# First batch's Fourier transform regrouped by TensorE transposes in place of a round trip through DRAM

## The chip, the cores and the metric

One core of a Trainium2 chip runs the whole program. The metric is device time in microseconds (us) of one execution; the number to compare is the median of several. The five engines are TensorE (PE, matrix multiplies into PSUM), VectorE (DVE), ScalarE (ACT), GpSimd (POOL) and SyncE (SP, which here only issues DMAs). Each engine works through its own instruction queue in order.

## What is computed

There are 8 batches of a 3072 x 256 float32 signal. Each is filtered in the frequency domain and the result goes through two dense layers and a soft mixture of experts:

```python
X = np.fft.rfft(x, axis=1)
y = np.fft.irfft(X * (filt_r + 1j * filt_i), n=3072, axis=1)
h = np.maximum(y.reshape(-1, 256) @ w_in, 0.0)          # 256 -> 2048
x2 = h * h @ w_out                                      # 2048 -> 256
logits = x2 @ phi                                       # 32 slots
# softmax over tokens gathers 32 slot inputs, 8 experts (w1, relu, w2) act on
# them, softmax over slots spreads the slot outputs back over the tokens
```

`w_in` and `w_out` arrive as float64 bit patterns and are turned into pairs of float32 on the chip.

## The kernel before

A transform over 3072 = 128 x 24 points is done in two steps. Step A multiplies by a 128-point matrix over the partition axis (`mm_a`, 12 pairs `u` of the 24 columns). Step B multiplies, for each of 64 frequencies, by a small matrix over the 24 columns (`mm_b`, 8 groups `i`), so the 24 columns have to move into the partition axis in between. The kernel does that through DRAM: `evac_a` copies a result of step A from PSUM to SBUF, `store_a` writes it to the DRAM tile `S`, and `load_s` reads it back with the axes exchanged. Then `filt` (DVE) and `join` (POOL) multiply by the filter, `mm_g` is the inverse of step B, `evac_g` (ACT) and `store_g` bring the group to the DRAM tile `G`, and `load_g` reads it with 4 columns per transfer for the inverse of step A (`mm_ai`, then `lead_ai` on ACT and `rest_ai` on DVE), which yields the input `xo` of the dense layers.

The first batch (b = 0) is a prologue: nothing else can run until its first 512 tokens are in `xo`. From then on pairs of dense-layer matrices (`pair`, `layer`) keep TensorE occupied, and the transforms of batches 1 to 7 are interleaved with them.

The order of the prologue is written by hand. `put0(t, fn)` files an event under a planned time `t`; the events are emitted in order of `t`, and each engine's queue gets its instructions in that order. The planned times are an order and no more: an engine waits until data, a buffer or a PSUM bank is there. The constants are `ST` (`B0`, `dB`: start and spacing of the filter groups; `G0`, `Gd`: start of `load_g` and of the step after it), `WI` (load and conversion of the 8 slices of `w_in`) and `WO` (the same for `w_out`).

One conversion of a `w_in` slice (`conv_wi`) is an ACT copy (k = 0), five DVE operations (k = 1 to 5), an ACT copy to `wiH` (k = 6) and a POOL subtraction to `wiL` (k = 7). Its input tile `wt` has 3 buffers, `wa` 3 and `we` 2. In the prologue the temporaries `f4` share 17 buffers of one tag, `u` shares 12, and PSUM tiles `sd` share 8 banks of one tag.

When the prologue is over, `open_main` exchanges the pools, and the first events of the main stream include `conv_wo(0, ...)`, whose `turn_wo` is a TensorE transpose that stands in TensorE's queue after the first two `layer` calls:

```python
WO = [((56.5, 57, W)[n] if n < 3 else W + 2 * n - 4.5,
       [W + max(2 * n + k - 1.5, 0) for k in (-1, -.5, 0, .5, 1, 1.5, 2, 2.5, 3.5, 4)]) for n in range(8)]
```

Of the kernel before, what the change touches and what calls it, by code (L numbers as in the profile page):

```python
# [6 lines left out]
F32 = mybir.dt.float32  # L7
# [8 lines left out]
D = 256  # L16
# [22 lines left out]
def body(tc, x, cA, cAf, fwd, inv, flt, cst, w_in, w_out, phi, w1, w2, out):  # L39
# [22 lines left out]
    def conv_at(t, act0, dve, hl):  # L62
        return [t + act0] + [t + d for d in dve] + [t + h for h in hl]

    SEQ = (.5, .6, .7, .8, .9)
    WI = [(t, conv_at(c, 0, SEQ, (1, 1.5))) for t, c in (
        (.9, 14), (12.1, 19), (24.2, 29.2), (28.2, 35.2), (34.2, 41.2), (40.2, 47.2), (46.2, 53.2), (52.2, 58.2)
    )]
    WO = [((56.5, 57, W)[n] if n < 3 else W + 2 * n - 4.5,
           [W + max(2 * n + k - 1.5, 0) for k in (-1, -.5, 0, .5, 1, 1.5, 2, 2.5, 3.5, 4)]) for n in range(8)]  # L70
    ev0 = defaultdict(list)

# [40 lines left out]
    def fft_events(b, pl, put, A0, dA, TB, TG, n, st):  # L113
        xv = x[b].rearrange("(p n) d -> p n d", n=N2)

        def big():
            return pl().tile([128, 4, D], F32, tag="f4", name="f4", bufs=n["f"])

        def small():
            return pl().tile([128, 2, D], F32, tag="u", name="u", bufs=n["u"])  # L120

        def load_x(sl):
            if b and sl % 2:
                t = st["x2"]
            else:
                t = wide() if b else big()
# [12 lines left out]

        def mm_a(u):  # L140
            p = side()
            if b == 0:
                a = 2 * (u % 2)
                pe.matmul(p, st["ca"], st["x", u // 2][:, a:a + 2, :], start=True, stop=True)
                st["a", u] = p
                return
            h, lo = st.pop(("xs", u))
            pe.matmul(p, ca_t[:, 0, :], h, start=True, stop=False)  # L148
            pe.matmul(p, ca_t[:, 1, :], h, start=False, stop=False)  # L149
            pe.matmul(p, ca_t[:, 0, :], lo, start=False, stop=True)  # L150
            st["a", u] = p

        def evac_a(u):
            if u == 0:
                st["S"] = dram.tile([N1, N2, D], F32, tag="S", name="S")
            p = st.pop(("a", u))
            o = small()
            act.activation(out=o, in_=p.rearrange("p (a d) -> p a d", d=D), func=ACTF.Copy)
            done(p)
            st["o", u] = o  # L160
            if b == 0:
                store_a(u)

        def store_a(u):
            sync.dma_start(out=st["S"][:, 2 * u:2 * u + 2, :], in_=st.pop(("o", u)))
# [5 lines left out]
        def load_w(i):  # L171
            st["fw", i] = w = pl().tile([128, 4, 2, 32], F32, tag="fw", name="fw", bufs=n["c"])
            for r in range(2):
                sync.dma_start(out=w[64 * r:64 * r + 48], in_=fwd[i, 64 * r:64 * r + 48])

        def load_v(i):
            st["iv", i] = v = pl().tile([128, 2, 2, 64], F32, tag="iv", name="iv", bufs=n["c"])
            sync.dma_start(out=v, in_=inv[i])

        def load_f2(j):  # L180
            st["f", j] = f = wide()
# [44 lines left out]
        def load_c(i):  # L226
            w = pl().tile([128, 4, 2, 32], F32, tag="fw", name="fw", bufs=n["c"])
            for r in range(2):
                sync.dma_start(out=w[64 * r:64 * r + 48], in_=fwd[i, 64 * r:64 * r + 48])
            v = pl().tile([128, 2, 2, 64], F32, tag="iv", name="iv", bufs=n["c"])  # L230
            sync.dma_start(out=v, in_=inv[i])
            st["fw", i], st["iv", i] = w, v

        def load_f(i):
            st["f", i] = f = big()
            sync.dma_start(out=f, in_=flt[i])

        def load_s(i):
            st["bi", i] = t = big()
            sv = st["S"].rearrange("(i r c h) n d -> i r (h n) c d", r=2, c=4, h=2)  # L240
            for r in range(2):
                sync.dma_start(out=t[64 * r:64 * r + 48], in_=sv[i, r])

        def mm_b(i):

            t, w = st.pop(("bi", i)), st.pop(("fw", i))
            st["p", i] = p = [side() for r in range(2)]
            for h in range(2):
                for c in range(4):
                    for r in range(2):  # L250
                        rows = slice(64 * r, 64 * r + 48)
                        pe.matmul(  # L252
                            p[r][32 * c:32 * c + 32, D * h:D * h + D], w[rows, c, h, :], t[rows, c, :],
                            start=True, stop=True, tile_position=(64 * r, 32 * c),
                        )

        def filt(i, r):

            p = st["p", i][r]
            f = st["f", i // 2][:, i % 2] if b else st["f", i]  # L260
            for k in range(2):
                st["uv", i, r, k] = u = small()
# [13 lines left out]

        def mm_g(i):
            v = st.pop(("iv", i))
            st["g", i] = p = [side() for c in range(4)]
            y = [st.pop(("y", i, r)) for r in range(2)]  # L280
            for k in range(2):
                for r in range(2):
                    for c in range(4):
                        rows = slice(32 * c, 32 * c + 32)
                        pe.matmul(
                            p[c][64 * r:64 * r + 64, 0:D], v[rows, r, k, :], y[r][rows, k, :],
                            start=(k == 0), stop=(k == 1), skip_group_check=True, tile_position=(32 * c, 64 * r),
                        )

        def evac_g(i, c):  # L290
            if c == 0:
                st["go", i] = big()
# [15 lines left out]

        def warm(a, n):

            p = side()
            w = a.shape[1]
            for _ in range(n):
                pe.matmul(p[:, 0:w], a[:, 0:128], a, start=True, stop=True)

        if b == 0:
# [3 lines left out]
            put(0, load_ca)  # L320
            put(0.05, warm, st["wz"], 2)
            put(0.05, warm, st["wz"][:, 0:256], 1)
            put(18.2, warm, st["ca"], 16)
            for sl in range(6):
                put(0.1 * sl + 0.2, load_x, sl)
            for u in range(12):
                put(4.6 + 0.9 * u, mm_a, u)
                put(6.7 + 1.0 * u, evac_a, u)
            for i in range(8):
                T = ST["B0"] + ST["dB"] * i  # L330
                put((.7, .75, 15)[i] if i < 3 else T - 6.5, load_c, i)
                put((.8, 9, 15.5)[i] if i < 3 else T - 6.4, load_f, i)
                put(18 + .1 * i if i < 3 else T - 6, load_s, i)
                put(T, mm_b, i)
                for r in range(2):
                    put(T + 1 + .5 * r, filt, i, r)
                    put(T + 1 + .5 * r, join, i, r)
                put(T + 5, mm_g, i)
                for c in range(4):
                    put(T + 6, evac_g, i, c)  # L340
                put(T + 7, store_g, i)
            return

        for sl in range(6):
# [458 lines left out]
    def load_const():  # L803
        gps.dma_start(out=ca_t, in_=cA)
        gps.dma_start(out=ss_t, in_=cst[:, C_SS:C_SS + 128])
        sync.dma_start(out=cst_t, in_=cst)
        sync.dma_start(out=phi_t, in_=phi.rearrange("(k p) s -> p k s", p=128))


# [25 lines left out]
    with tc.manual_schedule():  # L835
        put, late = stream("fft"), stream("late")
        st = {}
        put0(38, load_const)
        fft_events(0, lambda: first, put0, 0, 0, 0, 0, dict(f=17, u=12, c=4), st)
        out_events(0, st, late)  # L840
        def wput(t, *a):

# [275 lines left out]
def _constants():  # L1118
# [13 lines left out]
    a[:, 0] = 1.0  # L1132
    a[:, 1] = alt
    cA = np.stack(split(a), axis=1)
    ci = np.where(ri[None, :] == 0, np.cos(ph), -np.sin(ph)).T.copy()
    ci[0] = 1.0
    ci[1] = alt
# [63 lines left out]
    fwd = f2.reshape(8, 2, 4, 64, 2, 32).transpose(0, 1, 3, 2, 4, 5).reshape(8, 128, 4, 2, 32).astype(np.float32)  # L1201
    inv = i2.reshape(8, 2, 4, 32, 2, 64).transpose(0, 2, 3, 1, 4, 5).reshape(8, 128, 2, 2, 64).astype(np.float32)

    cst = np.zeros((128, C_END), np.float32)
    cst[:, C_I:C_I + 128] = ci * (2.0 / N)
# [5 lines left out]
    mats = (cA.astype(np.float32), a.astype(np.float32), fwd, inv)  # L1211
    return [np.ascontiguousarray(m) for m in mats], cst, ks


# [42 lines left out]
```

## Time and profile before

| | us |
|---|---|
| median of 3 runs | 1985.58 |
| lowest and highest | 1982.19, 1985.64 |
| the profiled execution | 1985.45 |
| its span, first to last instruction | 1983.7 |
| first matmul of a dense layer | 99.27 |

The span is what the trace covers; the rest of the profiled execution lies around it. Busy times in the views are sums over instructions of an engine. A row of a timeline or a chain gives the start in us from the beginning of the span, the length in us, and the instruction as engine, line, operation and tiles; "x4" means that four were merged, and what stands in brackets is the idle time ahead and its releaser. [...]

### The profile page before, as it was taken

The numbers are of one execution on the slowest core, as the hardware profiler recorded it, in microseconds if no ns is written. First come the engines' busy times: TensorE is split into PE (matmuls) and PEld (weight loads), VectorE is DVE, ScalarE is ACT, GpSimd is POOL, SyncE is SP. The second block draws the span as 40 slices with busy tenths as digits, with TensorE's granted clock in tenths as the row PEclk, the third lists the DMA queues.
The fourth block names the chain that finished last, engine by engine and source line by source line (L and its number), as shares of the span: only waits on it lengthen the run. The fifth ranks groups of instructions, "written<-read, shape, count | busy, mean of one in ns | idle before, by whom it ended". The sixth has DMA issues, their size and how long they took to land.

```text
span 1983.7 us, 44493 instructions
## 1 busy us (share of the span) xinstructions
PE 1919.6 (97%) x18318; PEld 1313.3 (66%) x18318; DVE 1194.6 (60%) x2230; ACT 1052.1 (53%) x1958; POOL 734.5 (37%) x786
## 2 busy tenths in 40 slices
PE   6799999999999999999999999999999999999987
PEld 3367667666767667667767667667667667676655
DVE  3675665666556655666456655666556656555658
ACT  2256456545645556545645556545655545454535
POOL 1515436343433344343433344343433332222224
PEclk7699999999999999999999999999999999999999
DMA  9833644441342424341342324341342314000589
GB/s 277 238 118 128 174 125 139 124 116 47 130 127 76 109 81 128 89 121 46 130 127 75 104 87 128 83 127 45 131 127 76 97 42 141 13 25 14 164 297 381
DMA packets 144762, 238.29 MB, mean 120 GB/s; under 512 B 14256, under 2 KB 96816, under 8 KB 144560
## 3 DMA queue, kind: packets, MB, share of 16 engines
q1 hardware_dynamic: 144272, 235.26, 39.1%
q8 instruction: 144, 2.36, 0.5%
q14 instruction: 58, 0.48, 0.1%
q0 software_dynamic: 288, 0.20, 0.1%
HBM read 154.66 MB, written 80.74 MB: 119 GB/s over the span
## 4 chain that ended last, share of the span: by engine, by line
PE 89%; DMA 4%; DVE 3%; ACT 2%; issue 2%; SPq 0%; ACTq 0%; DVEq 0%
PE p L442 19%; PE p L444 17%; PE p L443 17%; PE sd L579 10%; PE L L469 9%; PE sd L388 4%; PE sd L252 3%; PE sd L202 3%; DMA wx<-w 1%; PE sd L148 1%; PE sd L149 1%; PE sd L150 1%; DVE ct L912 1%; DMA f<-S 1%; PE pt L901 1%
## 5 line engine op out<-in xcount | busy, mean ns | idle before, releaser
L449 ACT ACTIVATE h<-p 128x512 f32<-128x512 f32 x768 | 459.0, 598 | 561.2 <-PE p L444 546.7
L453 POOL TENSOR_TENSOR h<-h 128x512 f32<-128x512 f32 x383 | 399.9, 1044 | 944.3 <-ACT h L449 899.3
L460 DVE STREAM_TRANSPOSE hT<-h 128x512 f32<-128x512 f32 x768 | 514.1, 693 | 331.0 <-ACT h L451 330.4
L442 PE MATMUL p<-xo,wiH 128*128 128x512 f32 x1536 | 629.5, 410 | 3.0 <-ACT h L449 2.3
L444 PE MATMUL p<-xo,wiL 128*128 128x512 f32 x1536 | 606.8, 395 | 0.0
L443 PE MATMUL p<-xo,wiH 128*128 128x512 f32 x1536 | 606.5, 395 | 0.0
L442 PEld LDWEIGHTS p<-xo,wiH 128*128 128x128 f32 x1536 | 289.6, 189 | 142.1 <-issue 69.9
L444 PEld LDWEIGHTS p<-xo,wiL 128*128 128x128 f32 x1536 | 289.3, 188 | 68.5
L443 PEld LDWEIGHTS p<-xo,wiH 128*128 128x128 f32 x1536 | 289.9, 189 | 57.0 <-DVE xo L409 0.4
L595 DVE SCALAR_TENSOR_TENSOR ac<-ac,sc,sd 128x512 f32<-128x512 f32 x184 | 129.7, 725 | 205.9 <-PE sd L579 205.9
L451 ACT ACTIVATE h<-h 128x512 f32<-128x512 f32 x385 | 243.3, 632 | 12.3
L579 PE MATMUL sd<-hT,eT 32*32 32x512 f32 x6144 | 214.2, 598 | 1.8 <-DVE eT L558 1.8
L272 POOL TENSOR_TENSOR u<-u 128x256 f32<-128x256 f32 x256 | 182.9, 745 | 78.5 <-DVE u L263 71.4
L469 PE MATMUL L<-h,wf 128*32 128x512 f32 x1536 | 186.0, 598 | 0.4 <-ACT h L451 0.4
L579 PEld LDWEIGHTS sd<-hT,eT 32*32 32x32 f32 x6144 | 101.6, 103 | 110.6 <-issue 56.6
L263 DVE TENSOR_TENSOR u<-sd,f 128x512 f32<-128x512 f32 x256 | 158.8, 678 | 21.8 <-PE sd L252 21.1
L137 POOL TENSOR_TENSOR u<-f,u 128x512 fp32r<-128x512 f32 x84 | 108.7, 1295 | 104.4 <-ACT u L136 103.0
L515 DVE TENSOR_TENSOR lo<-L,lp 128x512 fp32r<-128x512 f32 x47 | 32.5, 690 | 134.4 <-ACT lp L514 134.4
L388 PEld LDWEIGHTS sd<-cst_t,gin 128*128 128x128 f32 x768 | 101.4, 193 | 11.4 <-DMA gin<-G 3.2
L212 ACT ACTIVATE f<-sd 128x512 f32<-128x512 f32 x112 | 61.2, 609 | 84.7 <-PE sd L202 84.7
L388 PE MATMUL sd<-cst_t,gin 128*128 128x128 f32 x768 | 102.1, 276 | 2.6 <-DMA gin<-G 2.6
L469 PEld LDWEIGHTS L<-h,wf 128*32 128x32 f32 x1536 | 40.2, 109 | 93.5 <-issue 92.2
(126 smaller groups left out, 1483.1 us busy)
## 6 DMA issues: line engine op xcount, KB each, us to landing
f<-flt SPq DMA_DIRECT2D x28, 1024.0 KB, 6.1
f<-x SPq DMA_DIRECT2D x48, 512.0 KB, 4.9
S<-u SPq DMA_DIRECT2D x96, 256.0 KB, 2.3
f<-S SPq DMA_DIRECT2D x128, 192.0 KB, 7.0
G<-f SPq DMA_DIRECT2D x128, 192.0 KB, 3.1
gin<-G SPq DMA_DIRECT2D x48, 512.0 KB, 5.2
out<-w1t SPq DMA_DIRECT2D x47, 512.0 KB, 5.0
iv<-inv SPq DMA_DIRECT2D x64, 128.0 KB, 4.7
```

The source lines that it names most:

```text
L263: vec.tensor_tensor(out=u, in0=p.rearrange("p (h d) -> p h d", d=D), in1=f[:, 2 * r + k:2 * r + k + 1, :].to_broadcast([128, 2, D]), op=AL ...
L272: gps.tensor_tensor(out=a[:, h, :], in0=a[:, h, :], in1=b[:, 1 - h, :], op=ALU.add if h else ALU.subtract)
L388: pe.matmul(p[:, 128 * a:128 * a + 128], t[:, a, 128 * k:128 * k + 128], cI, start=True, stop=True,)
L442: pe.matmul(p, wh, x[:, 0, kk, :], start=(kk == 0), stop=False)
L443: pe.matmul(p, wh, x[:, 1, kk, :], start=False, stop=False)
L444: pe.matmul(p, wl, x[:, 0, kk, :], start=False, stop=(kk == 1))
L449: act.activation(out=h, in_=p, func=ACTF.Relu, scale=2.0 ** -8)
L451: act.activation(out=h, in_=h, func=ACTF.Square)
L453: gps.tensor_tensor(out=h, in0=h, in1=h, op=ALU.mult)
L460: vec.transpose(hT[c][:, 2 * i + k, :], h2[P, k])
L469: pe.matmul(lg[c][32 * n:32 * n + 32, :], wf[:, f, :], h2.pop((P + n // 2, n % 2)), start=(f < 4), stop=(f >= FT - 4), tile_position=(0, 3 ...
L579: pe.matmul(S[r][32 * t:32 * t + 32, :], e[rows, o:o + 32], h[rows, :, o:o + 32], start=(a == 0), stop=(a == 3), tile_position=(32 * r, 32 ...
```

## The change

The program computes the same. In the first batch the twelve `mm_a` become `mm_at`: the signal is now the stationary operand and the 128-point matrix (its columns reordered on the host, `cAf`) the moving one, so the result comes out with the 256 channels on the partitions; four 128-column multiplies per pair instead of one of 512. `evac_at` copies each result into one SBUF tile `AT`, in runs of two elements that lie 32 elements apart. After the twelfth, `mm_t` takes 4 transposes per half group (16 half groups) and `evac_t` copies each half group to SBUF, on ACT but for two on DVE. `store_a`, `load_s` and `S` are gone for this batch.

Tiles and PSUM banks of the prologue get names (`one`, `bank0`) in place of shared tags. The matrices of step B come in 2 loads of four groups (`load_c`), with a `memset` on POOL for the unused rows, and `mm_b` of this batch reads 64 rows instead of 48. The 16 warming multiplies with `ca` go. `cst` is loaded at the start. The conversions of `w_in` are spread otherwise: slices 0 and 1 ahead of the filters, slice 2 one DVE operation per group, slices 3 to 5 after the last filter, slices 6 and 7 (loaded after `load_g`) after `rest_ai` in DVE's queue. The layout of `fwd` and `inv` in DRAM changes for all batches.

```diff
-    ST = dict(B0=22, dB=4, G0=58.5, Gd=1.5)
+    ST = dict(F0=20.3, dF=2.9, G0=49, Gd=1.5)
+    WI = [
+        conv_at(.4, 8.6, 8.7, 12.3, 12.4),
+        conv_at(.7, 12.5, 12.6, 15.8, 15.9),
+        (1.35, [20.0] + [F(k + 1) + 2.45 for k in range(5)] + [F(6) + 4.4, 44.1]),
+        conv_at(27, 38, 44, 47.2, 47.3),
+        conv_at(30, 41, 47, 50, 50.1),
+        conv_at(36, 45, 50, 53, 53.1),
+        conv_at(49.1, 53.2, 56.5, 58.5, 58.6),
+        conv_at(52, 56.6, 59, 61, 61.1),
+    ]
+        def bank0(k):
+            return G["ps"].tile([128, 512], F32, tag=f"q{k}", name="sd", bufs=1)
+        def load_c(k):
+            w = one(f"fw{k}", [128, 4, 4, 2, 32])
+            v = one(f"iv{k}", [128, 4, 2, 2, 64])
+            gps.memset(w, 0.0)
+            for g in range(4):
+                o = 64 * (g // 2) + N2 * (g % 2)
+                sync.dma_start(out=w[32 * g:32 * g + N2], in_=fwd[k, o:o + N2])
+            sync.dma_start(out=v, in_=inv[k])
...
+        def mm_at(u):
+            st["at", u] = p = bank0(u % 8)
+            for k in range(2):
+                for m in range(2):
+                    o = 128 * (2 * k + m)
+                    pe.matmul(
                        p[:, o:o + 128], st["x", u // 2][:, 2 * (u % 2) + m, 128 * k:128 * k + 128], st["ca"],
...
+        def evac_at(u):
+            act.activation(
+                out=st["AT"][:, :, :, 2 * u:2 * u + 2], func=ACTF.Copy,
+                in_=st.pop(("at", u)).rearrange("p (k n q) -> p k q n", k=2, n=2),
+            )
+        def mm_t(i, s):
+            st["tp", i, s] = p = bank0((0, 4, 5, 6, 7)[2 * i + s] if 2 * i + s < 5 else 0)
+            for c in range(2):
+                for k in range(2):
+                    o, q = D * c + 128 * k, 16 * i + 8 * s + 4 * c
+                    a = st["AT"][:, k, q:q + 4, :].rearrange("p q n -> p (q n)")
+                    pe.transpose(p[:, o:o + 128], a, ident)
+        def evac_t(i, s):
...
+            if s and i < 2:
+                vec.tensor_copy(o, p)
+            else:
+                act.activation(out=o, in_=p, func=ACTF.Copy)
...
-            put(18.2, warm, st["ca"], 16)
+            put(0.35, lambda: sync.dma_start(out=cst_t, in_=cst))
             for sl in range(6):
-                put(0.1 * sl + 0.2, load_x, sl)
+                put((.2, .3, .5, .6, .8, .9)[sl], load_x, sl)
             for u in range(12):
-                put(4.6 + 0.9 * u, mm_a, u)
-                put(6.7 + 1.0 * u, evac_a, u)
+                put(5 + .95 * u, mm_at, u)
+                put(6.5 + .95 * u, evac_at, u)
+            put(1, load_c, 0)
+            put(1.6, load_c, 1)
             for i in range(8):
-                put(18 + .1 * i if i < 3 else T - 6, load_s, i)
-                put(T, mm_b, i)
+                put((1.1, 1.3, 1.4, 1.5)[i] if i < 4 else F(i - 4) + 2.6, load_f, i)
+                for s in range(2):
+                    T = F(i - 3) + 2.4 + 1.4 * s if i > 2 else 17.3 + .2 * i + .1 * s if i < 2 else F(0) - .3 + .1 * s
+                    put(T, mm_t, i, s)
+                    put(T + .5, evac_t, i, s)
+                put(F(i) - 1.5, mm_b, i)
                 for r in range(2):
+                    put(F(i) + 1.25 * r, filt, i, r)
+                    put(F(i) + 1.3 + 1.25 * r, join, i, r)
+                put(F(i + 1) + 2.85, mm_g, i)
                 for c in range(4):
+                    put(F(i + 1) + 3.7, evac_g, i, c)
+                put(F(i + 1) + 4.9, store_g, i)
```

## Rows read from the trace of the kernel before

**Rows 1.** The page, part 1: busy us, share of the span, instructions.
```profile
PE 1919.6 (97%) x18318; PEld 1313.3 (66%) x18318; DVE 1194.6 (60%) x2230; ACT 1052.1 (53%) x1958; POOL 734.5 (37%) x786
```

**Rows 2.** Windows: length, busy us (x instructions) by engine, TensorE clock, DMA share, GB/s.
```profile
5.00:10.00 5.00, 5.00 (x14) 2.47 (x13) 0.00 (x0) 2.45 (x5) 0.00 (x0) 1.00 1.01 404
20.00:25.00 5.00, 0.00 (x0) 0.00 (x0) 2.35 (x4) 2.09 (x4) 1.26 (x1) 0.70 1.05 401
30.00:35.00 5.00, 0.61 (x2) 0.17 (x2) 0.00 (x0) 0.00 (x0) 0.83 (x1) 0.50 0.58 127
35.00:39.00 4.00, 3.81 (x57) 1.68 (x62) 1.47 (x3) 0.00 (x0) 0.10 (x1) 0.50 1.13 179
34.00:80.00 46.00, 36.45 (x480) 14.22 (x480) 33.34 (x52) 11.93 (x33) 27.02 (x35) 0.57 0.99 261
200.00:300.00 100.00, 100.00 (x1203) 67.09 (x1202) 64.36 (x120) 48.25 (x88) 39.05 (x46) 1.00 0.53 148
```

**Rows 3.** The chain that ended last, 0 to 120 us: start, us, what.
```profile
37.62 9.43 DMA f<-S
...
87.18 0.30 SPq L303
...
87.53 3.45 DMA G<-f
91.13 5.27 DMA gin<-G
...
100.29 0.60 DVE xo L409
...
103.26 0.70 DVE wa L716
```

**Rows 4.** Timeline of SP's DMA queue, 0 to 13 us: start, us, what.
```profile
5.30 0.51 SPq L231 DMA_DIRECT2D iv<-inv  x1
...
12.49 0.38 SPq L662 DMA_DIRECT2D wt<-w_in  x1
```

**Rows 5.** Groups by line and shape, 0 to 105 us: busy, mean ns, idle before.
```profile
L272 POOL TENSOR_TENSOR u<-u 128x256 f32<-128x256 f32 x32 | 23.8, 778 | 9.3 <-DVE u L263 9.3
...
L263 DVE TENSOR_TENSOR u<-sd,f 128x512 f32<-128x512 f32 x32 | 19.7, 683 | 10.9 <-PE sd L252 10.8
...
L689 POOL TENSOR_TENSOR wiL<-wa,wiH 128x512 fp32r<-128x512 f32 x8 | 10.1, 1268 | 48.1 <-ACT wiH L687 43.0 <-DMA S<-u 5.1
...
L158 ACT ACTIVATE u<-sd 128x512 f32<-128x512 f32 x12 | 6.9, 594 | 6.3 <-PE sd L144 6.3
...
L673 ACT ACTIVATE wa<-wt 128x512 f32<-128x512 f32 x8 | 5.5, 683 | 8.0 <-DMA wt<-w_in 8.0
...
L687 ACT ACTIVATE wiH<-wa 128x512 fp32r<-128x512 f32 x8 | 5.0, 630 | 21.1 <-DVE wa L684 21.1
```

**Rows 6.** Timeline of TensorE and ScalarE, 15 to 110 us.
```profile
15.74 3.73 PE L314 MATMUL sd<-ca 128*128 128x128 f32 x32
...
42.96 1.96 PE L252 MATMUL sd<-f,fw 48*32 48x256 f32 x32
...
63.84 2.01 PE L285 MATMUL sd<-u,iv 32*64 32x256 f32 x32
...
76.06 1.21 ACT L294 ACTIVATE f<-sd 128x256 f32<-128x256 f32 x4 [4.82 <-PE sd L285]
...
104.00 1.11 PE L726 MATMUL sd<-cst_t,wa 128*128 128x128 f32 x4 [2.24 <-DVE wa L716]
...
109.72 0.60 PE L726 MATMUL sd<-cst_t,wa 128*128 128x128 f32 x4
```

**Rows 7.** Timeline of DVE, one w_in conversion and a contended one.
```profile
25.76 0.43 DVE L645 TENSOR_SCALAR wa<-wa 128x512 uint32<-128x512 uint32 x1 [3.31 <-ACT wa L673]
...
28.14 0.69 DVE L684 TENSOR_TENSOR wa<-wa,we 128x512 f32<-128x512 f32 x1
...
52.61 1.02 DVE L645 TENSOR_SCALAR wa<-wa 128x512 uint32<-128x512 uint32 x1
```

More of the change, by code (lines that the diff above doesn't have):

```diff
@@ L57, in body, with F, conv_at @@
     G["nsd"] = 8
-    ST = dict(B0=22, dB=4, G0=58.5, Gd=1.5)
+    ST = dict(F0=20.3, dF=2.9, G0=49, Gd=1.5)
     W = 1000
[L62 to L69, printed above, removed]
+    def F(i):
+        return ST["F0"] + ST["dF"] * i
+    def conv_at(t, a, d, h, lo):
+        return t, [a] + [d + .1 * k for k in range(5)] + [h, lo]
+    WI = [
[8 more added lines that the diff above has]
+    ]
+    WO = [((53.5, 56.7, W)[n] if n < 3 else W + 2 * n - 4.5,
            [W + max(2 * n + k - 1.5, 0) for k in (-1, -.5, 0, .5, 1, 1.5, 2, 2.5, 3.5, 4)]) for n in range(8)]
@@ L114, in fft_events, with one, small @@
         xv = x[b].rearrange("(p n) d -> p n d", n=N2)
-        def big():
-            return pl().tile([128, 4, D], F32, tag="f4", name="f4", bufs=n["f"])
-        def small():
+        def bank0(k):
+            return G["ps"].tile([128, 512], F32, tag=f"q{k}", name="sd", bufs=1)
+        def one(tag, shape):
+            return pl().tile(shape, F32, tag=tag, name=tag.rstrip("0123456789"), bufs=1)
+        def small(k=None):
+            if b == 0:
+                return one(f"u{k % 12}", [128, 2, D])
             return pl().tile([128, 2, D], F32, tag="u", name="u", bufs=n["u"])
@@ L125, in load_x @@
             else:
-                t = wide() if b else big()
+                t = wide() if b else one(f"x{sl}", [128, 4, D])
             if b:
@@ L173, in load_w @@
             for r in range(2):
-                sync.dma_start(out=w[64 * r:64 * r + 48], in_=fwd[i, 64 * r:64 * r + 48])
+                sync.dma_start(out=w[64 * r:64 * r + 48], in_=fwd[i // 4, 64 * r:64 * r + 48, i % 4])
         def load_v(i):
             st["iv", i] = v = pl().tile([128, 2, 2, 64], F32, tag="iv", name="iv", bufs=n["c"])
-            sync.dma_start(out=v, in_=inv[i])
+            sync.dma_start(out=v, in_=inv[i // 4, :, i % 4])
         def load_f2(j):
@@ L224, in store_g2 @@
                     sync.dma_start(out=gv[2 * j + k, r], in_=o[64 * r:64 * r + 48, k])
[L226 to L232, printed above, removed]
+        def load_c(k):
[6 more added lines that the diff above has]
+            sync.dma_start(out=v, in_=inv[k])
+            for i in range(4):
+                st["fw", 4 * k + i], st["iv", 4 * k + i] = w[:, i], v[:, i]
@@ L234, in load_f @@
         def load_f(i):
-            st["f", i] = f = big()
+            st["f", i] = f = one(f"f{i % 4}", [128, 4, D])
             sync.dma_start(out=f, in_=flt[i])
[L238 to L242, printed above, removed]
+        def mm_at(u):
[4 more added lines that the diff above has]
+                    pe.matmul(
+                        p[:, o:o + 128], st["x", u // 2][:, 2 * (u % 2) + m, 128 * k:128 * k + 128], st["ca"],
+                        start=True, stop=True,
+                    )
@@ L244, in mm_b @@
+        def evac_t(i, s):
+            if s == 0:
+                st["bi", i] = one(f"x{i % 3}", [128, 4, D])
+            o, p = st["bi", i][:, 2 * s:2 * s + 2, :], st.pop(("tp", i, s)).rearrange("p (c d) -> p c d", d=D)
+            if s and i < 2:
+                vec.tensor_copy(o, p)
+            else:
+                act.activation(out=o, in_=p, func=ACTF.Copy)
         def mm_b(i):
             t, w = st.pop(("bi", i)), st.pop(("fw", i))
-            st["p", i] = p = [side() for r in range(2)]
+            st["p", i] = p = [side() if b else bank0(1 + (2 * i + r) % 3) for r in range(2)]
@@ L250, in mm_b @@
                     for r in range(2):
-                        rows = slice(64 * r, 64 * r + 48)
+                        rows = slice(64 * r, 64 * r + (48 if b else 64))
                         pe.matmul(
@@ L261, in filt @@
             for k in range(2):
-                st["uv", i, r, k] = u = small()
+                st["uv", i, r, k] = u = small(4 * i + 2 * r + k)
                 vec.tensor_tensor(
@@ L278, in mm_g @@
             v = st.pop(("iv", i))
-            st["g", i] = p = [side() for c in range(4)]
+            st["g", i] = p = [bank0(4 + c) for c in range(4)]
             y = [st.pop(("y", i, r)) for r in range(2)]
@@ L291, in evac_g @@
             if c == 0:
-                st["go", i] = big()
+                st["go", i] = one(f"x{3 + i % 3}", [128, 4, D])
             p = st["g", i][c]
@@ L309, in warm @@
         def warm(a, n):
-            p = side()
+            p = bank0(7)
             w = a.shape[1]
@@ L322, in fft_events @@
             put(0.05, warm, st["wz"][:, 0:256], 1)
[L323 removed]
+            st["AT"] = one("AT", [128, 2, N1, 32])
+            put(0.04, lambda: vec.memset(st["AT"][:, :, :, N2:], 0.0))
+            put(0.35, lambda: sync.dma_start(out=cst_t, in_=cst))
             for sl in range(6):
[L325 removed]
+                put((.2, .3, .5, .6, .8, .9)[sl], load_x, sl)
             for u in range(12):
[L327 to L328 removed]
+                put(5 + .95 * u, mm_at, u)
+                put(6.5 + .95 * u, evac_at, u)
+            put(1, load_c, 0)
+            put(1.6, load_c, 1)
             for i in range(8):
[L330 to L334 removed]
+                put((1.1, 1.3, 1.4, 1.5)[i] if i < 4 else F(i - 4) + 2.6, load_f, i)
[4 more added lines that the diff above has]
+                put(F(i) - 1.5, mm_b, i)
                 for r in range(2):
[L336 to L338 removed]
+                    put(F(i) + 1.25 * r, filt, i, r)
+                    put(F(i) + 1.3 + 1.25 * r, join, i, r)
+                put(F(i + 1) + 2.85, mm_g, i)
                 for c in range(4):
[L340 to L341 removed]
+                    put(F(i + 1) + 3.7, evac_g, i, c)
+                put(F(i + 1) + 4.9, store_g, i)
             return
@@ L805, in load_const @@
         gps.dma_start(out=ss_t, in_=cst[:, C_SS:C_SS + 128])
-        sync.dma_start(out=cst_t, in_=cst)
         sync.dma_start(out=phi_t, in_=phi.rearrange("(k p) s -> p k s", p=128))
@@ L837, in body @@
         st = {}
-        put0(38, load_const)
-        fft_events(0, lambda: first, put0, 0, 0, 0, 0, dict(f=17, u=12, c=4), st)
+        put0(13, load_const)
+        fft_events(0, lambda: first, put0, 0, 0, 0, 0, None, st)
         out_events(0, st, late)
@@ L1199, in _constants @@
     i2[0, 24, 0], i2[0, 0, 1] = i2[0, 0, 1].copy(), 0.0
-    fwd = f2.reshape(8, 2, 4, 64, 2, 32).transpose(0, 1, 3, 2, 4, 5).reshape(8, 128, 4, 2, 32).astype(np.float32)
-    inv = i2.reshape(8, 2, 4, 32, 2, 64).transpose(0, 2, 3, 1, 4, 5).reshape(8, 128, 2, 2, 64).astype(np.float32)
+    fwd = f2.reshape(8, 2, 4, 64, 2, 32).transpose(0, 1, 3, 2, 4, 5).reshape(2, 4, 128, 4, 2, 32)
+    fwd = fwd.transpose(0, 2, 1, 3, 4, 5).astype(np.float32)
+    inv = i2.reshape(8, 2, 4, 32, 2, 64).transpose(0, 2, 3, 1, 4, 5).reshape(2, 4, 128, 2, 2, 64)
+    inv = inv.transpose(0, 2, 1, 3, 4, 5).astype(np.float32)
     cst = np.zeros((128, C_END), np.float32)
@@ L1210, in _constants @@
     cst[:, C_M4:C_M4 + 4] = (r[:, None] // NS) == np.arange(4)[None, :]
-    mats = (cA.astype(np.float32), a.astype(np.float32), fwd, inv)
+    mats = (cA.astype(np.float32), cAf.astype(np.float32), fwd, inv)
     return [np.ascontiguousarray(m) for m in mats], cst, ks
```

9 lines of the change are left out of this document (2 added, 7 removed).

## The prediction

> **What bounds the kernel now.** The page first: TensorE is busy 97% of the span [rows 1], so time can come only from where it is not. The windows by stretch say where: from 200 us on it is busy without a gap at the full clock, while in the prologue it stands still (0 of 5 us from 20 to 25, 0.61 of 5 from 30 to 35) and runs at a mean granted clock of 0.57 from 34 to 80 [rows 2]. What the main stream does after the prologue isn't touched, so I take the kernel's time as the length of the prologue plus a constant.
>
> Inside the prologue the chain of waits names the order: the round trip through S, still 9.43 us of waiting for a read of S at 37.62, then the filter groups, the last store into G issued at 87.18, its landing, the load of `gin`, `rest_ai` ending at 100.9, and the conversion of the first `w_out` slice, which ends at 103.96 and releases `turn_wo` [rows 3]. The DMA engines are full meanwhile, share 0.99 at 261 GB/s from 34 to 80 and 1.13 at only 179 GB/s from 35 to 39, where the 1 KB rows of S are read, against 404 GB/s from 5 to 10 with the 4 KB rows of x [rows 2]. I call the issue of the last store into G "E". It is 87.2 now; the sum needs E after the change and what lies behind it.
>
> **The change part by part.**
>
> *Loads of x.* By the code the tenth transfer in SP's queue goes out at 5.30 and the fifteenth at 12.49 [rows 4]. I read that as at most 8 in flight, each issue waiting for the landing eight places ahead: x's first 512 KB land at 5.30 and its sixth at 12.49, 1.44 us apiece. Now two `w_in` slices and `cst` (216 KB) stand between them, 7.4 pieces in place of 5: the last lands at 5.3 + 7.4 x 1.44 = 16.0 (with nothing added 12.5, at a quarter worse 18.6).
>
> *Step A.* Four 128-column multiplies per pair, two instructions each. 32 such instructions took 3.73 us at full clock, 0.117 each [rows 6], so 0.93 per pair; the last two pairs end at 17.9. An evacuation of 128x512 takes 0.594 [rows 5]: 18.6. Nothing in the trace writes runs of two elements 32 apart. Nearest is the copy that reads every second element, 0.683 against 0.630 for its contiguous neighbour [rows 5]; I take no penalty, because ACT has 0.93 per pair to do 0.6, and keep 1.2 (double) as the other end. Memsets and the 64-row `mm_b` lie in idle time of DVE and POOL or in unchanged columns: 0. The early conversions 0 and 1 use DVE and ACT while they wait for x: 0.
>
> *Regrouping.* Four transposes took 0.60 at full and 1.11 at half clock [rows 6]. The first four half groups: 2.4, to 21.0. `mm_b` took 1.96 at half clock [rows 6]; halved, with a tail, 1.2: the first filter starts at 22.2.
>
> *Filter groups.* Per group, by the rows' means: DVE 4 x 0.683 = 2.7, in five groups also one conversion operation, 0.43 alone and 1.02 while POOL works [rows 5, 7]; POOL 4 x 0.778 = 3.1 [rows 5]; TensorE at full clock 2 x 0.6 + 1.0 + 1.0 = 3.2; ACT 1.2 + 1.21 = 2.4 [rows 5, 6]. Longer than each is a loop through one PSUM bank: from the sixth half group on all transposes use bank 0, and by the written order the first half's transposes (0.6) go ahead of `mm_g` (1.0), whose four evacuations (1.21) stand in ACT's queue ahead of the second half's (0.6), which must free the bank: with three handovers of 0.1, 3.7 us. Five groups carry it: 18.5. Two before it at 2.8 and the last at 2.7: 8.3. The last filter ends at 22.2 + 26.8 = 49.0.
>
> *To E.* Last join 2 x 0.778 = 1.6; then ACT holds `evac_g` behind the copy of conversion 5, which needs the buffer that `wiL` of slice 2 on POOL frees: 1.27 + 0.68 [rows 5]; four evacuations 1.21; handovers 0.3. E = 54.0, against 87.2: 33.2 saved.
>
> *Behind E.* G's landing, `gin` and `mm_ai` cost what they did; conversions 3 to 5 (3 x 3.07, from 25.76 to 28.83 [rows 7]) fit in those 14 us. But conversions 6 and 7 now stand behind `rest_ai` on DVE and ahead of the first `w_out` conversion, which TensorE's third group of instructions waits for: 2 x 3.07 = 6.1, and 0.6 for a stretch beside POOL's `wiL`. The copy of slice 6 stands ahead of `lead_ai` on ACT and waits for a load issued behind `gin`: 0.3. Lost: 7.0 (6.1 to 8).
>
> Loads of `fwd` and `inv` for the later batches keep their 1 KB rows and are asked for well ahead; 0.
>
> **Sum.** 33.2 - 7.0 = 26.2. The profiled execution took 1985.45, 0.1 from the median: 1985.45 - 26.2 = 1959. The forecast's own range, groups of 3.0 at best and of 4.2 with late loads at worst, is 1952 to 1965.
>
> **Rivals.**
>
> *Half clock in the filter groups.* After 18.6 us everything on TensorE takes its half-clock time: 16 x 1.11 + 8 x 1.96 + 8 x 2.01 = 49.6 us [rows 6], back to back, plus some 5.5 for the last filter, join and evacuation: E = 73.7, 13.5 saved, 1979. For it: the clock fell to 0.70 and 0.50 after TensorE stood still at 20 us, and was half in most of the old filter stage [rows 2]. Against: the new order leaves no such pause, and transposes took 0.60 at full clock inside the main stream [rows 6]. [...] Chance 0.14.
>
> *Slow evacuations of step A.* At 1.2 us apiece ACT sets step A: from 6.4 (5.3, a pair's 0.93 and a handover) 12 x 1.2, and 2 x 0.68 + 2 x 0.63 for the conversions' copies, give 23.4 in place of 18.6: 1964. [...] Chance 0.13.
>
> *The DMA engines stay the bound.* Up to E the new order moves 15.6 MB (x 3.1, filters 4.2, six slices 3.1, matrices 1.9, G 2.8, the rest 0.5). At the 261 GB/s of the old filter stage that is 60 us, E = 62, 1967: chance 0.07. The other side: at the 179 GB/s of the stretch of 1 KB rows it is 87, E = 89 and, with the 7.0 behind E, 1994. It decides below 190 GB/s, where E passes 84. Only G is left in 1 KB rows, and 4 KB rows moved at 404 [rows 2], so 0.03.
>
> *The gain doesn't reach the end*, because the main stream waits for something else, later `w_out` slices say, whose loads now wait for slices 6 and 7: 1985. Against it the gapless windows [rows 2]. Chance 0.03.
>
> **How the numbers follow.** The forecast 1959 has 0.55 and a better outcome, below 1952, 0.05; with the rivals' 0.14, 0.13, 0.10 and 0.03 that is 1. A range from 1952 to 1974 leaves out the better outcome and most of the half clock. Two executions differ by about 0.2%, 4 us, so this is what counts as no change: faster 0.94, same 0.03, slower 0.03.
>
> **What would show it.** Right: x's last load lands near 16; the first filter at 22, filters ending near 49 at a granted clock near 1; no transfer of S; E near 54; DVE busy for some 9 us between `rest_ai` and the first `turn_wo`; from there rows as before. Wrong: evacuations of step A well over 0.6; a granted clock of 0.5 between 20 and 45; SP's queue or `evac_t` waiting for a load; filter groups over 4.5 us apart; a gap in the main stream that was not there.

## The result and the profile after

The changed kernel takes 1960.77 us (median of 4 runs, 1959.98 to 1961.14), the kernel before beside it 1985.36 (1982.19 to 1985.64): ratio 0.9879, 95% interval 0.9862 to 0.9896, so 1.2% faster. The forecast was 1959, with 1952 to 1965 as its own range. The profiled execution took 1960.66, 24.8 less than that of before.

Part 1 of the page of the changed kernel (busy us, share of the span, instructions) answers to [rows 1]: TensorE keeps its 97%, of a span 24.9 us shorter.

```profile
PE 1909.2 (97%) x18422; PEld 1319.0 (67%) x18422; DVE 1201.8 (61%) x2233; ACT 1059.8 (54%) x1972; POOL 738.1 (38%) x788
```

Its windows, with the columns of [rows 2]; the granted clock is a share of TensorE's full speed. The filter stage now runs at the full clock (1.00), with TensorE busy 21.92 of 24 us; the stretch between `xo` and the first `turn_wo` is where TensorE stands, 4.67 of 16 us busy; the main stream is as full as it was.

```profile
20.75:24.00 3.25, 3.25 (x24) 2.92 (x30) 0.70 (x2) 1.46 (x3) 0.00 (x0) 0.50 1.12 384
...
25.00:49.00 24.00, 21.92 (x469) 12.49 (x466) 23.07 (x36) 14.49 (x37) 21.36 (x29) 1.00 0.90 274
...
64.00:80.00 16.00, 4.67 (x25) 3.60 (x24) 12.72 (x20) 5.87 (x11) 3.58 (x3) 0.74 0.40 123
200.00:300.00 100.00, 99.70 (x1078) 68.48 (x1070) 62.60 (x116) 57.72 (x109) 51.27 (x57) 1.00 0.53 151
```

Its chain of waits (start, us, what) answers to [rows 3]. Where the reads of S stood there is now a loop on the chip: transposes, `mm_g`, four evacuations, one evacuation, next transposes. From the last filter to `rest_ai` the chain runs through conversions 3 to 5 on DVE and the load of slice 6 and not through G. Further down the stretch behind `rest_ai` has grown.

```profile
34.13 0.66 PE sd L270 x4
34.79 1.15 PE sd L322 x32
35.94 1.19 ACT x L331 x4
...
37.68 0.66 PE sd L270 x4
...
59.73 5.26 DMA wt<-w_in
64.98 0.58 ACT xo L439
65.59 1.29 DVE xo L451 x2
...
73.08 0.70 DVE wa L726
74.34 0.65 ACT wa L747
75.02 1.06 DVE wa L687
...
78.01 0.70 DVE wa L758
78.76 1.12 PE sd L768 x4
```

Rows of its timeline (start, us, instruction, and the idle time ahead with its releaser): the first operation of conversion 1, the load of a `w_in` slice that is issued when x's last load lands, the last two evacuations of step A and the row that holds them up, the first transposes, the first filter, POOL's `wiL` of slice 2 with a DVE operation beside it and the copy that waits for it, the evacuation that ends at E (the store is issued 0.03 us later), the inverse of step A, the copy of slice 6, and one contended operation of conversion 7.

```profile
15.05 1.03 DVE L687 TENSOR_SCALAR wa<-wa 128x512 uint32<-128x512 uint32 x1 [1.26 <-ACT wa L715]
...
15.81 0.38 SPq L704 DMA_DIRECT2D wt<-w_in  x1
...
18.76 0.63 ACT L729 ACTIVATE wiH<-wa 128x512 fp32r<-128x512 f32 x1 [2.07 <-DVE wa L726]
19.30 1.08 ACT L259 ACTIVATE AT<-sd 128x512 f32<-128x512 f32 x2
...
20.43 3.52 PE L270 MATMUL sd<-cst_t,AT 128*128 128x128 f32 x16 [2.47 <-ACT AT L259]
...
25.13 5.08 DVE L300 TENSOR_TENSOR u<-sd,f 128x512 f32<-128x512 f32 x8 [0.45 <-PE sd L289]
...
52.28 1.45 POOL L731 TENSOR_TENSOR wiL<-wa,wiH 128x512 fp32r<-128x512 f32 x1
52.64 1.64 DVE L692 SCALAR_TENSOR_TENSOR we<-wt,we 128x512 f32<-128x512 uint32 x1
53.76 0.69 ACT L715 ACTIVATE wa<-wt 128x512 f32<-128x512 f32 x1 [1.70 <-POOL wiL L731]
...
54.33 1.22 ACT L331 ACTIVATE x<-sd 128x256 f32<-128x256 f32 x4
...
63.55 1.95 PE L430 MATMUL sd<-cst_t,gin 128*128 128x128 f32 x16
...
64.39 0.68 ACT L715 ACTIVATE wa<-wt 128x512 f32<-128x512 f32 x1 [0.88 <-DMA wt<-w_in]
...
70.95 1.37 DVE L691 TENSOR_SCALAR we<-wa 128x512 uint32<-128x512 uint32 x1
```

Its groups by line and shape, 0 to 105 us (busy, mean ns, idle before), answer to [rows 5]:

```profile
L309 POOL TENSOR_TENSOR u<-u 128x256 f32<-128x256 f32 x32 | 24.7, 806 | 6.9 <-DVE u L300 6.8
L300 DVE TENSOR_TENSOR u<-sd,f 128x512 f32<-128x512 f32 x32 | 19.8, 681 | 1.2 <-issue 0.5 <-PE sd L289 0.5
...
L259 ACT ACTIVATE AT<-sd 128x512 f32<-128x512 f32 x12 | 7.2, 616 | 6.9 <-PE sd L253 6.8
```

The regrouping evacuation costs 616 ns against 594 for the plain one. In the filter stage DVE now hardly waits (1.2 us in 32 operations, 10.9 before).

Everything the change moved lies ahead of the last `turn_wo`. It starts at 141.91 us in the trace before and at 116.64 after, 25.3 earlier; the time fell by 24.8.

```profile
141.91 0.63 PE L726 MATMUL sd<-cst_t,wa 128*128 128x128 f32 x4 [0.93 <-DVE wa L716]
```

```profile
116.64 0.63 PE L768 MATMUL sd<-cst_t,wa 128*128 128x128 f32 x4 [0.93 <-DVE wa L758]
```

Profiled time less that start is 1843.5 and 1844.0, and between 1842.9 and 1844.7 in all profiled executions of this study. So below I read a version from where its prologue and first pairs end.

### The profile page after: what moved, and what is told of

Same layout as the page of the kernel before. It is cut to its first block, busy times and chain, and to the rows that moved or that the text cites. A ratio compares the mean times of both kernels' runs of the same rounds, so it can differ in the third digit from the quotient of the medians.

```text
span 1958.8 us, 44662 instructions
## 1 busy us (share of the span) xinstructions
PE 1909.2 (97%) x18422; PEld 1319.0 (67%) x18422; DVE 1201.8 (61%) x2233; ACT 1059.8 (54%) x1972; POOL 738.1 (38%) x788
## 4 chain that ended last, share of the span: by engine, by line
PE 91%; DVE 4%; ACT 2%; issue 2%; DMA 0%; ACTq 0%; DVEq 0%
PE p L484 19%; PE p L486 17%; PE p L485 17%; PE sd L621 11%; PE L L511 9%; PE sd L430 4%; PE sd L289 3%; PE sd L209 3%; PE sd L157 1%; PE sd L158 1%; PE sd L159 1%; DVE ct L953 1%; PE pt L942 1%; ACT h L491 1%; PE pt L1142 1%
```

## The experiments

Every experiment computes the same. Ratios are to the kernel before on the same chip, with 95% intervals. "Filters" is the start of the first filter operation to the end of the last.

**The round trip put back (e1_dram).** All of the change but its point: step A, S and its reads as before, the rest (conversions, names, early `cst`) kept.

```diff
-                put(5 + .95 * u, mm_at, u)
-                put(6.5 + .95 * u, evac_at, u)
+                put(5 + .95 * u, mm_a0, u)
+                put(6.5 + .95 * u, evac_a0, u)
...
-                for s in range(2):
+                put(F(i - 3) + 2.4 if i > 2 else 17.3 + .1 * i, load_s, i)
+                for s in ():
```

> The changed kernel with one part undone: the first batch's regrouping goes through the DRAM tile S again (512-column multiplies of step A, one store per pair, two loads per group); order of conversions, named banks and buffers, spacing of events as changed. If the round trip and its transfers were the cost that the change removed, the stores queue behind the early loads on SP, the first filter starts near 39 instead of 25, the last store into G is issued at 72 to 80 instead of 56, and the time is 1976 to 1986. If instead the gain came from the order of the conversions and the named buffers, the last store stays within 3 us of 56 and the time within 1959 to 1964.

1986.87 us, ratio 1.0016 (1.0007 to 1.0025): without the regrouping the change gains nothing; by the interval it is slower by 0.07 to 0.25%. Filters 43.48 to 75.52, with a mean granted clock of 0.70 from 44 to 80, E at 81.12, first `turn_wo` at 103.91: the first filter and E come later than expected, and the time lies 0.9 us above the expected range. The chain of waits of this kernel shows a filter load, then the round trip, stores and a read of S:

```profile
15.92 10.79 DMA f<-flt
...
26.77 5.81 DMA S<-u
32.65 4.57 DMA S<-u
...
39.19 4.87 DMA x<-S
```

Against before, E comes 6.0 earlier and `rest_ai` ends 9.0 earlier (92.0), and then the conversions behind `rest_ai` take all of it back: the first `turn_wo` starts 0.1 earlier. Against the changed kernel E is 25.6 later. That is what the regrouping is worth in this order of loads, with the clock that came with it (1.00 in the changed kernel's filter stage, 0.70 here from 44 to 80). Not all of it is the round trip as the kernel before had it: here the stores to S stand behind filter loads in SP's queue, and the first filter starts some 6 us later than before (43.48 against 37.53). An order that keeps S and puts the stores ahead of these loads was not run, so how much of those 6 us could be had without the regrouping stays open.

**The conversions put back between the filter groups (e2_conv).**

```diff
-        (1.35, [20.0] + [F(k + 1) + 2.45 for k in range(5)] + [F(6) + 4.4, 44.1]),
-        conv_at(27, 38, 44, 47.2, 47.3),
...
-        conv_at(52, 56.6, 59, 61, 61.1),
+        conv_at(1.35, 20.0, F(1) + 2.45, F(1) + 3, F(1) + 3.1),
+        conv_at(22, F(2) + 2.4, F(3) + 1.3, F(3) + 1.9, F(3) + 2),
...
+        conv_at(38, F(7) + 3.2, F(8) + 2, F(8) + 5, F(8) + 5.1),
```

> The changed kernel with the other part undone: slices 2 to 6 of w_in are converted between the filter groups, all five DVE operations at once, and slice 7 after the last group, so that nothing of w_in is left behind rest_ai. If DVE then paces the groups, five conversions of 3.1 to 4 us take the place of one: the last store into G moves from 56 to about 70, the stretch from rest_ai to the first w_out transpose shrinks from 11.9 to about 3, and the time is 1965 to 1970. If the place of the conversions is a wash, 1959 to 1962. If what stands behind rest_ai costs more than what stands between the groups, under 1959.

1965.29 us, ratio 0.9908 (0.9893 to 0.9922). Filters 23.40 to 59.97, E at 70.47. `rest_ai` to first `turn_wo` is 3.0 us again (81.42 to 84.45). The filter stage holds four conversions more than in the changed kernel and takes 36.6 us in place of 24.7, 3.0 more for each. So a conversion between the groups lengthens the filter stage one for one, since DVE has hardly any idle time there (busy 23.07 of 24 us in the changed kernel), and one behind `rest_ai` lengthens that stretch. The new placement is the better by 4 to 5 us (1965.29 less the changed kernel's 1960.1 to 1960.9), because conversions 3 to 5 lie where G is on its way and DVE has nothing else.

**Conversions 6 and 7 in the main stream (e3_defer, e3_again; e8_later two steps later still).** Their DVE operations are filed behind the first `w_out` conversions; `wt` gets 5 buffers (6 in e8_later).

```diff
-        conv_at(49.1, 53.2, 56.5, 58.5, 58.6),
-        conv_at(52, 56.6, 59, 61, 61.1),
+        conv_at(W + 1.6, W + 6.1, W + 6.2, W + 7.1, W + 7.2),
+        conv_at(W + 4, W + 8.1, W + 8.2, W + 9.1, W + 9.2),
```

> The changed kernel with slices 6 and 7 of w_in loaded and converted inside the main stream, after the first three w_out conversions (5 input buffers instead of 3). If the 8.9 us that the stretch from rest_ai to the first w_out transpose has grown by are all lost, the transpose comes about 8.5 us earlier and the time is 1952 to 1955. The rival: DVE is the bound of the first pairs of the main stream (97% busy from 78 to 100), so the two conversions cost the same 6 us there: 1959 to 1961. Between: 1955 to 1959, half given back.

> As e3_defer, with both conversions 2 steps later in the main stream (6 input buffers), as late as the sixth and seventh slice allow. If DVE's total work up to the eighth pair is what counts, their place inside the stretch changes nothing: 1955 to 1958, the eighth w_out transpose near 111.6 as in e3_defer. If it matters how far each stands behind the w_out conversions, another 1 to 2 us come off.

> e3_defer once more, with more executions, on the chip of this call: 1954.5 to 1958, about 3.5 us under the changed kernel's 1960.

> The changed kernel once more beside it, as the yardstick of this chip, with the same number of executions: 1958 to 1962.

| | median us | runs from, to | ratio (interval) |
|---|---|---|---|
| e3_defer | 1956.92 | 1954.55, 1958.35 | 0.9865 (0.985 to 0.988) |
| e3_again | 1956.75 | 1955.18, 1958.46 | 0.9865 (0.985 to 0.988) |
| e8_later | 1956.44 | 1955.39, 1957.68 | 0.9865 (0.9849 to 0.9882) |
| changed kernel beside the last two (c_again) | 1960.90 | 1959.11, 1964.57 | 0.9888 (0.9873 to 0.9903) |

The first `turn_wo` starts at 69.18 in e3_again and at 78.37 in c_again: 9.2 us. The last starts at 112.97 and 116.17: only 3.2 of them are left. The timeline of TensorE in e3_again shows where they go:

```profile
69.18 0.66 PE L768 MATMUL sd<-cst_t,wa 128*128 128x128 f32 x4 [2.25 <-DVE wa L758]
...
83.18 0.63 PE L768 MATMUL sd<-cst_t,wa 128*128 128x128 f32 x4 [0.32 <-DVE wa L758]
93.19 1.08 PE L768 MATMUL sd<-cst_t,wa 128*128 128x128 f32 x4 [5.70 <-DVE wa L758]
101.71 0.60 PE L768 MATMUL sd<-cst_t,wa 128*128 128x128 f32 x4
```

and so does a window, where DVE is busy 18.33 of 20 us and TensorE 13.98:

```profile
80.00:100.00 20.00, 13.98 (x70) 9.32 (x69) 18.33 (x29) 9.44 (x18) 5.97 (x5) 0.83 0.44 136
```

The first pairs of the main stream are DVE's as well: every pair waits there for a `w_out` conversion, and two more conversions among them make two gaps. In e8_later the gaps stand two steps later (87.01 to 96.67 to 104.65) and are nearly as long. About 6 of the 9 us come back as waits. Not all of the 3.2 that are left belongs to the move: in c_again's trace the clock fell ahead of the first transposes (0.52 from 20 to 22, 1.00 in e3_again), and its first filter starts 1.3 later than e3_again's (24.84 against 23.58). Against c_after (below), whose clock did not fall there (1.00 from 18 to 30), the first `turn_wo` is 7.8 earlier (69.18 against 77.01) and the last 2.1 (112.97 against 115.09). So 2 to 3 us are kept by the traces, and 4.2 by the medians of e3_again and c_again. e3_again and e8_later are the best versions seen: their runs, beside the changed kernel's on the same chip, don't overlap with its runs, though the intervals of the ratios do. 0.2% is what this measurement can just tell.

**The last evacuations freed (e4_head).** The `wiH` copy of slice 1 is filed behind them.

```diff
-        conv_at(.7, 12.5, 12.6, 15.8, 15.9),
+        conv_at(.7, 12.5, 12.6, 17.05, 17.1),
```

> The changed kernel with one event moved: the ACT copy that ends conversion 1 stands behind the last evacuation of step A instead of ahead of the last two. If that copy is what stopped TensorE from 18.0 to 20.4 and brought its clock down to half until 24.0, the last evacuation ends near 18.7, the clock stays at 1.0, the first filter starts near 22.5 instead of 25.1 and the time is about 1958. The rival: the filters and slice 2 land at 20.4 to 23.7 and hold the first groups anyway, gain under 1 us: 1960 to 1961.

1961.02 us, ratio 0.9889 (0.9872 to 0.9905): nothing gained. Rows of TensorE's and of ScalarE's timeline in this kernel:

```profile
17.40 2.02 PE L253 MATMUL sd<-ca,x 128*128 128x128 f32 x16 [0.80 <-DMA x<-x]
```

```profile
18.56 0.62 ACT L259 ACTIVATE AT<-sd 128x512 f32<-128x512 f32 x1 [1.32 <-PE sd L253]
19.46 0.60 ACT L259 ACTIVATE AT<-sd 128x512 f32<-128x512 f32 x1 [0.27 <-PE sd L253]
...
25.10 0.76 ACT L715 ACTIVATE wa<-wt 128x512 f32<-128x512 f32 x1 [2.83 <-DMA wt<-w_in]
```

The evacuations no longer wait for `wiH` but for step A itself, whose last multiplies wait 0.80 us for x's last load here, and end at 20.06 in place of 20.38. The clock stays at 1.00 (20 to 24) and the first filter starts at 23.19, no earlier than in c_after, which has the copy in its old place (23.26). Then ACT stands 2.8 us at the copy of slice 2, which waits for its load. With the copy out of the way, the loads hold the same place in this execution; since x came late, it doesn't show what the move gains where x is on time.

**The changed kernel as yardstick (c_after) and its loop (e5_loop).** In e5_loop the four evacuations of `mm_g` stand behind the second half's evacuation in ACT's queue, so that bank 0 is free earlier.

```diff
-                    put(F(i + 1) + 3.7, evac_g, i, c)
+                    put(F(i + 1) + 4.35, evac_g, i, c)
```

> The changed kernel itself, as the yardstick of this chip. In its first profile the clock was half from 20.7 to 24.0 and the first filter started at 25.1; two variants with the same head started theirs at 23.4 and 23.7 at full clock after a pause of the same kind. If the fall of the clock is a matter of the execution, this one may start it anywhere from 23.2 to 25.2; the time should be 1958 to 1961.

> The changed kernel with the four evacuations of mm_g moved behind the second half's evacuation on ACT. If the loop through PSUM bank 0 and those four evacuations sets the 3.54 us between filter groups, the next bound is TensorE's own work, 3.3 us, and five groups give 1.2 us: the last store into G about 1 us earlier, time 1957 to 1960. The rival: DVE or POOL (2.5 to 3.4 and 3.1 to 3.3 us per group) take over at once and nothing moves, or the later evacuations push mm_g back and the groups get longer.

c_after: 1960.11 us, ratio 0.9881 (0.9866 to 0.9896); first filter at 23.26. e5_loop: 1962.41, ratio 0.9893 (0.9876 to 0.9909). The groups stay 3.48 us apart. DVE's timeline in e5_loop:

```profile
35.66 2.48 DVE L300 TENSOR_TENSOR u<-sd,f 128x512 f32<-128x512 f32 x4 [0.31 <-issue]
38.06 1.03 DVE L692 SCALAR_TENSOR_TENSOR we<-wt,we 128x512 f32<-128x512 uint32 x1
39.14 2.48 DVE L300 TENSOR_TENSOR u<-sd,f 128x512 f32<-128x512 f32 x4
```

Filters and one conversion operation, back to back, are 3.5 us: with the loop shortened DVE is the bound at once. E came 1.2 us later (54.82 against 53.63), since the last group's evacuations now stand behind the `wiH` copy of slice 3, which waits for DVE.

**Slice 6 while G is on its way, slice 7 in the main stream (e7_best).** With e5's edit, and `wt` with 5 buffers.

```diff
-        conv_at(49.1, 53.2, 56.5, 58.5, 58.6),
-        conv_at(52, 56.6, 59, 61, 61.1),
+        conv_at(40, 50.2, 53.2, 56, 56.1),
+        conv_at(W + 4, W + 8.1, W + 8.2, W + 9.1, W + 9.2),
```

> The changed kernel with what the runs so far point to: slice 6 of w_in loaded ahead of load_g (5 input buffers) and converted by DVE while G drains, slice 7 loaded and converted in the main stream, and the evacuations of mm_g behind the second half's. If DVE's idle stretch ahead of rest_ai (some 3 us) takes most of one conversion, this keeps what the deferral of both gave (about 4 us) and adds 2 to 4: 1951 to 1954. The rival: the conversion delays rest_ai by as much as it frees later, 1955 to 1957.

1957.76 us, ratio 0.9869 (0.9854 to 0.9884). E moves to 55.73 and DVE is busy without a break from 48.8 to 66.3. A fourth conversion doesn't fit in that time with the other three, so it pushes what follows. The time is above both ranges expected, and no better than e3_again's.

**The clock held up through the round trip (e6_warm).** The kernel before, with more warming multiplies.

```diff
-            put(18.2, warm, st["ca"], 16)
+            put(18.2, warm, st["ca"], 80)
```

> The kernel before with 80 warming multiplies in place of 16 behind step A, so that TensorE has no pause up to the first filter group. If the transfers pace the old prologue, the first groups run at full clock and the last store into G is still issued within 2 us of 87; time as before. The rival, that half the gain is the clock: the last store comes 6 us or more earlier.

One run of 1979.5 us, beside 1983.67 (median of 7, 1982.53 to 1985.10) for the kernel before. The granted clock is 1.00 until 39 us (0.50 before), as the window with the extra multiplies shows, and 0.70 from 34 to 80 in place of 0.57 [rows 2].

```profile
26.00:34.00 8.00, 8.00 (x72) 7.70 (x70) 1.57 (x3) 0.63 (x1) 1.27 (x1) 1.00 0.65 183
```

The first filter comes 2.0 us earlier, E 2.9, so between the two cases expected, and the time of this one run lies below all seven of the kernel before. Behind E the lead grows: the first `turn_wo` is 5.2 earlier than in the trace before and the last 6.7 (141.91 there).

```profile
98.82 0.66 PE L726 MATMUL sd<-cst_t,wa 128*128 128x128 f32 x4 [2.24 <-DVE wa L716]
...
135.20 0.63 PE L726 MATMUL sd<-cst_t,wa 128*128 128x128 f32 x4 [0.93 <-DVE wa L716]
```

`mm_ai` (2.05 us in place of 3.18) and this first `turn_wo` (0.66 in place of 1.11) take here about what they take at a granted clock of 1.00 (1.95 in the changed kernel, 0.66 in e3_defer); whether the added multiplies did that, one run doesn't show. So a clock held up to 39 us was worth 2 to 3 us of the old stage. It was half again for much of the rest (0.50 from 50 to 60, 0.70 in the mean), so what a full clock throughout would have given stays open.

**Transposes alone and the clock (t1_clock).** In the changed kernel 48 transposes take the place of the 7 warming multiplies that bridge the wait for G.

```diff
-            for _ in range(7):
-                pe.matmul(p[:, 0:416], cI, cst_t[:, 0:416], start=True, stop=True)
+            for k in range(48):
+                pe.transpose(p[:, 128 * (k % 4):128 * (k % 4) + 128], cI, ident)
```

> The changed kernel with 48 transposes of a 128x128 constant in place of the 7 warming multiplies ahead of mm_ai, so that TensorE comes out of its pause with nothing but transposes. In the first profile the clock came back at 24.0, 3.6 us after TensorE resumed with 16 transposes and before or just as mm_b began; with multiplies it came back 3.3 to 6 us after. If transposes count as work for the clock gate, it rises to 1.0 within 3 to 6 us of the first and the rest of them take 0.15 us each. If they do not count, it stays at 0.5 through all 48 (13 us) and into mm_ai, and rest_ai ends some 4 us later.

One run of 1960.01 us, and in its timeline and windows (the clock stands third from the end):

```profile
55.51 8.33 PE L423 MATMUL sd<-cst_t 128*128 128x128 f32 x48 [2.35 <-ACT x L331]
```

```profile
55.00:61.00 6.00, 5.49 (x26) 5.49 (x27) 5.79 (x8) 1.61 (x4) 2.93 (x2) 0.50 0.46 111
61.00:61.50 0.50, 0.50 (x5) 0.50 (x4) 0.47 (x2) 0.00 (x0) 0.05 (x1) 0.56 0.89 270
61.50:64.00 2.50, 2.50 (x25) 2.50 (x24) 1.25 (x2) 0.63 (x1) 0.47 (x1) 1.00 1.03 392
```

The clock went from half to full 5.9 us after the first transpose, with nothing but transposes on TensorE. With the multiplies it took 3.2 us (c_after) to 6.0 (the changed kernel).

## Why the prediction was right

By its own steps, with what the profile after showed:

| step | predicted | measured |
|---|---|---|
| x's last load has landed | 16.0 | 15.8 |
| last evacuation of step A ends | 18.6 | 20.4 |
| first filter | 22.2 | 25.1 (23.0 to 23.7 in eight others) |
| length of the filter stage | 26.8 | 24.7 |
| last filter to E | 5.0 | 5.8 |
| E | 54.0 | 55.55 |
| saved up to E | 33.2 | 31.6 |
| E to end of `rest_ai`, against before | 0 | 2.5 gained |
| `rest_ai` to first `turn_wo`, against before | 7.0 lost | 8.9 lost |
| sum | 26.2 | 25.2 |

*The round trip* was the cost, as the sum had it. e1_dram shows it from the other side: with S back, in the order of loads of the change, nothing of the gain is left. The clock up to the first filters was not it (e6_warm: 2.9 us of E). How the 25.6 us of e1_dram divide into waits for S and the lower clock that was measured with them (0.50 from 39 to 44, 0.70 from 44 to 80), no run separates.

*Step A* was mis-sized by 1.8 us. The loads came on time and the evacuation's price was right; what the working left out is the queue. The last two evacuations stand on ACT behind `wiH` of slice 1, which waits for a DVE conversion whose first operation took 1.03 us in place of 0.43 beside POOL's `wiL` of 1.28. That is 0.6 of the 1.8; for the rest, conversion 1 starts only behind conversion 0, whose `wiH` stands on ACT ahead of the copy of slice 1. This is read from the trace; e4_head, where x's last load came later, doesn't confirm it. "They wait for x" covered the early conversions in the first part of step A, not at its end.

*Regrouping* took 3.5 us in place of 2.4 in the profiled execution, as the clock fell to half 0.2 us after the first transpose. Three executions show a fall there (the profiled one, c_again, t1_clock); TensorE had stood for 2.33 to 2.47 us before. The eight others, with 0.69 to 2.26 us, show 1.97 us for the 16 transposes at full clock. It costs 1.2 to 2.1 us at the first filter between any two of these traces, less than the runs scatter in the time (1959.11 to 1964.57 in c_again).

*Filter groups.* The loop through bank 0 is there as forecast: 3.54 us apart at 34.13, 37.68 and 41.22, against 3.7, and the chain runs round it. But it carries three groups, not five. Groups 0 and 1 go at 2.5 each, and the next two at 3.3, set by DVE with its conversion operation. So the stage was 2.1 shorter, and hid most of the late start. e5_loop shows that the loop and DVE's own work are nearly equal.

*To E.* The path is the one forecast: POOL's last joins, its `wiL` of slice 2, the copy of slice 5 on ACT, four evacuations. But the joins end 2.5 us after the last filter in place of 1.6, and `wiL` took 1.45 beside DVE in place of 1.27.

*Behind E.* DVE ran conversions 6 and 7 where the prediction put them, 66.80 to 73.77, 7.0 us with the contention against 6.1 + 0.6. Not in the sum: the copy of the first `w_out` slice stands behind `wiH` of slice 7 on ACT, so DVE waits 1.24 more, and then its first operation takes 1.05, in place of 0.42, beside POOL's `wiL` of 1.27. From E to `rest_ai` 2.5 us came back: `gin` is issued 0.7 sooner after E and lands 1.2 sooner (4.1 us after its issue, 5.3 before); `mm_ai`, behind its warming multiplies, starts 0.6 after that and takes 1.95 at the full clock in place of 3.18. The copy of slice 6 does hold `lead_ai`: ACT waits 0.88 for its load, and `lead_ai` starts at 64.98, some 0.4 after the first half of `mm_ai` (an estimate: half of 1.95 from 63.55). By so much the path through G was the shorter one. The errors, 1.6 up to E, 1.9 and −2.5, nearly cancel, and within the 1.6 a first filter 2.9 late is offset by the 2.1 of the filter stage. That the sum is better than its terms is luck.

*The rivals.* Half clock in the filter groups: refuted, 1.00 from 25 to 49 (its rows add up to 49.5 us, not 49.6, which moves nothing). With transposes alone on TensorE the clock rose too, 5.9 us after the first (t1_clock). Slow evacuations: refuted, 616 ns; a ScalarE copy with both strides takes 22 ns more than the plain one's 594. DMA as the bound: the engines are nearly as full as before (0.90 at 274 GB/s from 25 to 49), but the transfers of the filter groups' results wait for ACT and no operation of the loop waits for a load. Ahead of the loop one does: in c_after the copy of slice 2 waits 1.57 us for its load with the third group's evacuations behind it (2.83 in e4_head). A gain that doesn't reach the end: in the changed kernel it does, 25.3 of the last `turn_wo` and 24.8 of the time. It is what befell the experiments on the late conversions: of 9.2 us at the first `turn_wo`, 3.2 reach the last (of 7.8, 2.1 against c_after).

What stays open: whether the few us between e3_again and an order in which no conversion holds up a pair can be had. e7_best, the one attempt beyond moving them, did not get there. Open too is what the new order with S, but with its stores ahead of the filter loads, would take.

## What to carry to other kernels

A stall that the chain names is worth what the next bound leaves: follow the new order by hand, engine by engine and bank by bank, and take the longest loop; here that gave the group spacing to 0.2 us in the three groups that the loop set. The errors came from in-order queues: for each instruction on the path, list what stands ahead of it on its engine and what that waits for, the last pieces of a stage above all. Work that is moved off one stall keeps only what the place it goes to has idle; a move by 8 to 9 us into pairs that DVE already set kept 2 to 4.

## What the runs showed of the hardware

- DVE's operations in the conversions, which read and write SBUF alone, took longer beside POOL in the changed kernel: one of 0.43 us (at 67.97) took 1.37 (at 70.95) while POOL's 1.45-us subtraction ran, and one of 0.69 (at 68.43) took 1.64 (at 52.64). `filt`, with an operand in PSUM, took 681 and 692 ns in the two operations that ended before POOL's first join, and 673 to 692 in the others.
- Reading PSUM out of order and writing pairs of elements 32 apart took ScalarE 616 ns in the mean of twelve (the changed kernel), the plain copy 594 (the kernel before).
- In t1_clock the granted clock went from 0.50 to 1.00 with transposes alone on TensorE, 5.9 us after the first. With multiplies, the return after the pause at E took from 3.2 us (c_after) to 6.0 (the changed kernel) in executions of the same program.
